# mLSTM cell and cosine-gated MLP on one core: the upper half of each w_in piece sent by GpSimd's queue

## The chip, the cores and the metric

One core of one Trainium2 chip runs the whole kernel in one launch. The metric is device time in microseconds. In the profile PE is TensorE, PEld its weight loads, DVE is VectorE, ACT is ScalarE, POOL is GpSimd and SP is SyncE, which here only issues DMAs; SPq and POOLq are the instruction queues of SP and GpSimd. L171 is line 171 of the kernel before; the change moves no line.

## The reference

Two blocks follow each other. The first is an mLSTM cell over 4 batches, 8 heads, 768 steps and a head size of 40:

```python
for t in range(S):
    m_new = np.maximum(f[t] + m, i[t])
    f_stab, i_stab = np.exp(f[t] + m - m_new), np.exp(i[t] - m_new)
    C = f_stab * C + i_stab * outer(v[t], k[t]);  n = f_stab * n + i_stab * k[t];  m = m_new
    y[t] = sigmoid(o[t]) * (C @ q[t]) / np.maximum(np.abs(n @ q[t]), 1.0)
```

The second takes the result as 3072 tokens of 320 features: `h = x @ w_in` (320 by 2048), `g = h * cos(h)`, `out = g @ w_out` (2048 by 320). The two weight matrices arrive as 64-bit floats, so the kernel loads each number as a pair of 32-bit words and makes a 32-bit float of it.

## The kernel before, in words

The sequence is cut into 6 chunks of 128 steps; with 4 batches that makes 24 cells, n = 4c + b for chunk c and batch b. A cell loads its q, k and v, forms scores (L481), weighs them with decay factors E (L404, L487), multiplies with values and state (L507 to L516), normalizes and turns the result (L525 to L536) into xT, the token features with features on partitions; the last 64 of the 320 features go into a second tile, xL, by two GpSimd DMAs for each cell of chunks 1 to 5 (L605). When a chunk of xT is whole, the MLP's first product, `Up(c, f2)`, runs for f2 = 0 to 7: four matmuls a half on xT with `w_in_sb` (L648) and one on xL with `w_in_l` (L642), into PSUM tiles pup; then the cosine gate on ACT and DVE (L656 to L668) and the second product (L680 in chunk 0, L758 later).

The order on every engine is written out by hand. `first_cells` sets up the gates and runs the cells of chunk 0; `both_parts(c, b)` then puts the MLP of chunk c beside the cells of chunk c + 1.

**How w_in comes in.** w_in is loaded in four pieces of 512 of its 2048 columns, by `weights_in(f)`, f = 0 to 3. A piece has two tiles of raw words. `bits` (partitions 0 to 127) takes 256 features, in four DMAs of 32 partitions, 256 KB each (L171). `low` takes the last 64 features, in four DMAs of 64 KB: two into partitions 0 to 63 and two into 64 to 127 (L176). All eight are issued by SP. Then `to_float32` converts: two ACT passes (L149, L151), three DVE passes (L155, L156, L162), one GpSimd pass that adds the two parts (L163), into `w_in_sb` (two slices of 512 columns) and `w_in_l`. w_out comes in eight pieces (L182) by the same conversion, as `w_out_sb`.

`weights_in(0)` stands in `first_cells` after the load of cell 3, `weights_in(1)` and `weights_in(2)` later in it, `weights_in(3)` in the first `both_parts`. A piece's instructions stand in the queue that issues them at that place, among that engine's other work. The tile `bits` has two buffers, shared with the decay factors of cell 3 (`E3`): piece 0 takes the second, piece 1 the first as soon as cell 3's value product (L497) has read E3, piece 2 the second again when piece 0 is converted, piece 3 the first. `low` shares two buffers with the first gates' tile in the same manner.

Other work on GpSimd that the steps below name: `kw`, the weighed keys (L409), needed by the state's increment on PE (L599); the triangular mask of E (L390), needed by the exponential on ACT (L400 or L404); `vr`, a copy of odd values (L415), and `qG`, the scaled queries (L463), both needed by the value product on PE (L510 to L516); the state's fade (L582); and the DMAs of the gates' tables to DRAM and back: `M_d` (L221, L247), `G_d` (L260), which SP reads again as E (L353) and G (L359).

SP's other loads are q and k (L326, L338), k and v for the state (L343), output gates o (L301, L308). A semaphore serves every eighth DMA of a kind of queue, so a DMA is issued when the eighth before it has landed; GpSimd's DMAs have eight such semaphores of their own.

Of the kernel before, what the change touches and what calls it, by code (L numbers as in the profile page):

```python
# [29 lines left out]
def kernel(  # L30
# [20 lines left out]
    nc = tc.nc  # L51
# [114 lines left out]
    w_in_last = moe_w_in.bitcast(I32).rearrange("(h d) (a e n) -> e a h d n", d=D, e=2, n=2 * 128)[:, :, :, 32:D]  # L166

    def weights_in(f):
        bits = pb.tile([128, NK, WP, 2], I32, name="bits", tag="bits")
        for a in range(HP):  # L170
            nc.sync.dma_start(out=bits[32 * a:32 * a + 32].rearrange("r i n two -> r i (n two)"),  # L171
                              in_=w_in_heads[a, 0:32, :, ts(f, 2 * WP)])
        low = p2.tile([128, 2 * 128, 2], I32, name="low", tag="S")
        for e in range(2):
            for a in range(2):
                nc.sync.dma_start(out=low[64 * e:64 * e + 64, ts(a, 128)].rearrange("r n two -> r (n two)"), in_=w_in_last[e, 2 * f + a])  # L176
        return [(w_in_sb[:, i, ts(f, WP)], bits[:, i]) for i in range(NK)] + [(w_in_l[:, ts(f, 2)].rearrange("p a n -> p (a n)"), low)]


# [652 lines left out]
    def first_cells():  # L832
# [29 lines left out]
        load_o(0, (2, 3))  # L862
        load(3)
        pieces.extend(weights_in(0))
        wall_in(1, 0, psum_o())
        wall_in(1, 1, psum_o())
# [55 lines left out]
        to_float32(pieces.pop(0))  # L922
        decay_exponents(B)
        pieces.extend(weights_in(1))
        outs.extend((p, weights_out(p)) for p in range(1, 3))
        seam_out(2)
# [15 lines left out]
        state(3)  # L942
        load_E(B + 2)
        ahead.append(weights_in(2))
        decay(B)
        sigmoid(1)
# [158 lines left out]
```

## Time and profile before

| | |
|---|---|
| median of 3 runs | 539.55 us (538.5 to 540.12) |
| the profiled execution: its time, its span | 540.26 us, 538.5 us |
| PE busy | 522.8 us (97%) |
| DVE busy | 419.5 us (78%) |
| ACT busy | 287.1 us (53%) |
| POOL busy | 247.8 us (46%) |
| hardware DMA queue (q1) | 96240 packets, 55.64 MB |
| software DMA queue (q0) | 1424 packets, 1.49 MB |

The time of the profiled execution is 1.8 us longer than its span, for what lies around it. The hardware queue is what SP issues (and one DMA of ACT), the software queue what GpSimd issues. Every part of w_in is loaded and converted in the first 119 us of the span; after that the change touches no instruction.

### The profile page before, as it was taken

To read this page: it belongs to the slowest core of one execution; us is meant where nothing else is said; L and a number is where in the kernel's file an instruction comes from. 1 tells how busy PE (TensorE), PEld (TensorE's weight loads), DVE (VectorE), ACT (ScalarE), POOL (GpSimd) and SP (SyncE) were. 2 spreads that over 40 slices of the span, in tenths; PEclk is the share of its full clock that TensorE was granted. 3 is DMA by queue.
4 is the path that set the end of the run, shared out by engine and by line. 5 is a ranking of instruction groups with operands and counts; after the bars stand their busy time and mean duration, and the time that the engine had idled before them with its cause. 6 is when DMAs were issued, how large, how long until landed. Compare 5 with 4: busy or idle time off the path is not lost.

```text
span 538.5 us, 10486 instructions
## 1 busy us (share of the span) xinstructions
PE 522.8 (97%) x3844; PEld 354.4 (66%) x3844; DVE 419.5 (78%) x907; ACT 287.1 (53%) x546; POOL 247.8 (46%) x409
## 2 busy tenths in 40 slices
PE   7999979999999999999999999999999999999996
PEld 4885536556666757767767767767657667576755
DVE  5565879897888988898878898878898879663636
ACT  2587949767566537827527826527836522222221
POOL 7435465465665865553553553553432433121211
PEclk9585989999999999999999999999999999999999
DMA  9999969799727539229249229159220000000001
GB/s 137 210 197 231 254 176 179 200 194 215 131 94 174 58 94 193 51 87 194 34 125 175 38 91 195 28 124 167 44 83 7 1 5 6 20 30 1 1 0 49
DMA packets 97762, 57.81 MB, mean 107 GB/s; under 512 B 62048, under 2 KB 89792, under 8 KB 97712
## 3 DMA queue, kind: packets, MB, share of 16 engines
q1 hardware_dynamic: 96240, 55.64, 50.4%
q0 software_dynamic: 1424, 1.49, 1.3%
q8 instruction: 30, 0.49, 0.4%
q14 instruction: 20, 0.16, 0.1%
q10 hardware_dynamic: 48, 0.02, 0.0%
HBM read 51.71 MB, written 4.11 MB: 104 GB/s over the span
## 4 chain that ended last, share of the span: by engine, by line
PE 76%; DMA 10%; DVE 8%; SPq 3%; POOL 2%; ACT 1%; issue 1%; DVEq 0%; POOLq 0%
PE pup L648 27%; PE acc L758 22%; PE pup L642 8%; PE po L680 5%; PE ps L481 3%; DMA bits<-in_moe_w_in_dram 3%; PE late L758 3%; PE vt L516 2%; PE vt L507 2%; DVE t L454 1%; DMA low<-in_moe_w_in_dram 1%; PE pu L599 1%; DMA G<-G_d 1%; DMA bits<-in_moe_w_out_dram 1%; DVE g L668 1%; DMA E<-M_d 1%
## 5 line engine op out<-in xcount | busy, mean ns | idle before, releaser
L648 PE MATMUL pup<-xT,w_in_sb 128*128 128x512 f32 x384 | 178.3, 607 | 4.0 <-POOL w_in_sb L163 2.9
L656 ACT ACTIVATE n<-pup 128x512 int32<-128x512 f32 x96 | 54.1, 595 | 201.7 <-PE pup L642 148.8
L648 PEld LDWEIGHTS pup<-xT,w_in_sb 128*128 128x128 f32 x384 | 70.7, 192 | 91.3 <-issue 84.4
L659 DVE SCALAR_TENSOR_TENSOR n<-pup,n 128x512 f32<-128x512 f32 x96 | 63.1, 687 | 79.6 <-ACT n L656 77.9
L722 POOL TENSOR_TENSOR D<-g 128x128 f32<-128x128 f32 x40 | 19.6, 490 | 138.0 <-DVE g L668 138.0
L664 ACT ACTIVATE n<-n 128x512 f32<-128x512 f32 x96 | 59.3, 630 | 16.0 <-DVE n L659 16.0
L668 DVE SCALAR_TENSOR_TENSOR g<-pup,n 128x512 f32<-128x512 f32 x96 | 62.0, 685 | 2.4 <-ACT n L664 1.7
L758 PE MATMUL acc<-w_out_sb,g 128*128 128x160 f32 x320 | 58.6, 304 | 0.0
L758 PE MATMUL acc<-T,g 128*128 128x160 f32 x320 | 58.0, 301 | 0.1
L642 PE MATMUL pup<-xL,w_in_l 64*128 64x512 f32 x192 | 55.7, 651 | 0.6 <-POOL w_in_l L163 0.6
L605 POOL DMA_DIRECT2D xL<-xT x40 | 22.4, 561 | 72.6 <-DVE xT L536 68.6
L758 PEld LDWEIGHTS acc<-w_out_sb,g 128*128 128x128 f32 x320 | 47.8, 190 | 5.6 <-issue 3.9
L758 PEld LDWEIGHTS acc<-T,g 128*128 128x128 f32 x320 | 48.1, 190 | 3.7 <-issue 3.0
L404 ACT ACTIVATE E<-E,tab 128x128 f32<-128x128 f32 x160 | 49.0, 389 | 0.3
L680 PE MATMUL po<-w_out_sb,g 128*128 128x320 f32 x128 | 36.2, 436 | 0.0
L481 PEld LDWEIGHTS ps<-t,t 40*128 40x128 f32 x384 | 26.4, 198 | 13.5 <-DVE t L454 7.2
L758 PE MATMUL acc<-T,S 128*128 128x160 f32 x160 | 35.0, 301 | 0.0
L680 PEld LDWEIGHTS po<-w_out_sb,g 128*128 128x128 f32 x128 | 24.0, 190 | 11.2 <-issue 1.9
L487 DVE TENSOR_TENSOR E<-ps,E 128x512 f32<-128x512 f32 x48 | 30.7, 681 | 0.5 <-PE ps L481 0.5
L642 PEld LDWEIGHTS pup<-xL,w_in_l 64*128 64x128 f32 x192 | 15.0, 187 | 24.5 <-issue 21.3
L481 PE MATMUL ps<-t,t 40*128 40x128 f32 x384 | 28.7, 289 | 1.1 <-DVE t L454 0.8
L758 PE MATMUL acc<-w_out_sb,S 128*128 128x160 f32 x160 | 28.8, 299 | 0.0
(177 smaller groups left out, 908.6 us busy)
## 6 DMA issues: line engine op xcount, KB each, us to landing
E<-M_d SPq DMA_DIRECT2D x22, 512.0 KB, 3.7
qr<-in_q_dram SPq DMA_DIRECT2D x36, 160.0 KB, 3.5
kr<-in_k_dram SPq DMA_DIRECT2D x36, 160.0 KB, 5.7
G<-G_d SPq DMA_DIRECT2D x20, 256.0 KB, 6.6
bits<-in_moe_w_out_dram SPq DMA_DIRECT2D x8, 640.0 KB, 6.8
bits<-in_moe_w_in_dram SPq DMA_DIRECT2D x16, 256.0 KB, 6.9
out_dram<-o_sb SPq DMA_DIRECT2D x24, 160.0 KB, 1.9
ks<-in_k_dram SPq DMA_DIRECT2D x10, 320.0 KB, 7.9
```

Source lines behind the costliest of these rows:

```text
L404: nc.scalar.activation(out=Es[n][:, h], in_=Es[n][:, h], func=AF.Exp, scale=-1.0, bias=tab[:, c, 0, g:g + 1])
L481: nc.tensor.matmul(ps[j][:, p], kT[r, p], qT[r, p], start=True, stop=True)
L487: nc.vector.tensor_tensor(out=w, in0=pss[n][j], in1=w, op=OP.mult)
L605: nc.gpsimd.dma_start(out=xL[c][64 * e:64 * e + 64, b], in_=ys[n][0:128:2])
L642: nc.tensor.matmul(pu, w_in_l[r, f2], xL[c][r].rearrange("p b t -> p (b t)"), start=ahead, stop=not ahead)
L648: nc.tensor.matmul(pu.rearrange("p (b t) -> p b t", b=B), w_in_sb[:, i, ts(2 * f2 + e, 128)], xT[c][:, i:NK * B:NK], start=(i == 0 and not ...
L656: nc.scalar.activation(out=self.n[e], in_=self.pu[e], func=AF.Copy, bias=0.25)
L659: nc.vector.scalar_tensor_tensor(out=self.n[e].bitcast(FP), in0=self.pu[e], scalar=0.25, in1=self.n[e], op0=OP.add, op1=OP.subtract)
L664: nc.scalar.activation(out=r, in_=r, func=AF.Sin, scale=TWO_PI_DOWN)
L668: nc.vector.scalar_tensor_tensor(out=g, in0=self.pu[e], scalar=TWO_PI, in1=self.n[e].bitcast(FP), op0=OP.mult, op1=OP.mult)
L680: nc.tensor.matmul(po[c][b], gs[c, f][:, ts(b, C)], w_out_sb[:, f], start=(f == 0), stop=(f == NF - 1))
L758: nc.tensor.matmul(a, lhs, rhs, start=start, stop=stop)
```

## The change

Of each piece, the `bits` DMAs with a = 2 and 3 (partitions 64 to 127) and the `low` DMAs with e = 1 (partitions 64 to 127) are issued by GpSimd instead of SP. Nothing else is edited. In the built program the order of PE, DVE and ACT stays as it was. SP has 16 DMAs less, GpSimd 16 more, four for each piece.

```diff
     def weights_in(f):
         bits = pb.tile([128, NK, WP, 2], I32, name="bits", tag="bits")
         for a in range(HP):
-            nc.sync.dma_start(out=bits[32 * a:32 * a + 32].rearrange("r i n two -> r i (n two)"),
+            (nc.sync, nc.gpsimd)[a // 2].dma_start(out=bits[32 * a:32 * a + 32].rearrange("r i n two -> r i (n two)"),
                               in_=w_in_heads[a, 0:32, :, ts(f, 2 * WP)])
         low = p2.tile([128, 2 * 128, 2], I32, name="low", tag="S")
         for e in range(2):
             for a in range(2):
-                nc.sync.dma_start(out=low[64 * e:64 * e + 64, ts(a, 128)].rearrange("r n two -> r (n two)"), in_=w_in_last[e, 2 * f + a])
+                (nc.sync, nc.gpsimd)[e].dma_start(out=low[64 * e:64 * e + 64, ts(a, 128)].rearrange("r n two -> r (n two)"), in_=w_in_last[e, 2 * f + a])
```

Where the four DMAs stand on GpSimd: piece 0's behind `kw` of cell 0 and ahead of the DMA of M_d (L247); piece 1's behind the mask of cell 4 (L390) and ahead of piece 0's second L163; piece 2's behind piece 0's third L163 and ahead of `kw`, `vr`, `qG` and the mask that follow; piece 3's behind the L163 of w_out's second piece and ahead of `qG`, `kw` and the mask.

## The prediction

> **What bounds the kernel now.** I read the page first: busy times and the chain that ended last.
>
> ```profile
> PE 522.8 (97%) x3844; PEld 354.4 (66%) x3844; DVE 419.5 (78%) x907; ACT 287.1 (53%) x546; POOL 247.8 (46%) x409
> PE 76%; DMA 10%; DVE 8%; SPq 3%; POOL 2%; ACT 1%; issue 1%; DVEq 0%; POOLq 0%
> ```
>
> PE is busy 97% of the span, so the change can at most act on 15.7 us of idle PE and on stretches at half clock. The waits of PE put its idle time almost wholly ahead of 75 us: 3.8 us before the first matmul, 2.9 us at 71.3 us (for L163 of w_in_sb), 0.9 us at 68.4 us. Later no gap is over 0.6 us. But DMA has 10% of the chain, so next the chain in order of time, in its first 75 us:
>
> ```profile
> 25.02 7.36 DMA low<-in_moe_w_in_dram
> 33.07 6.96 DMA G<-G_d
> 40.61 0.68 ACT w_in_sb L149
> ...
> 47.57 5.78 DMA bits<-in_moe_w_in_dram
> 53.36 6.79 DMA bits<-in_moe_w_out_dram
> 60.17 11.73 DMA bits<-in_moe_w_in_dram
> 71.93 0.70 DVE w_in_sb L162
> 72.77 1.33 POOL w_in_sb L163
> 74.14 2.56 PE pup L648 x4
> ```
>
> By this, w_in's transfers set the first PE gap. I don't take it on trust: does DVE stand still for a DMA at 71.9? Its timeline:
>
> ```profile
> 70.79 0.29 DVE L156 TENSOR_SCALAR w_in_l<-w_in_l 128x256 int32<-128x256 int32 x1
> 71.00 0.49 DVE L155 TENSOR_SCALAR w_out_sb<-w_out_sb 128x640 f32<-128x640 f32 x1
> 71.53 0.49 DVE L156 TENSOR_SCALAR w_out_sb<-w_out_sb 128x640 int32<-128x640 int32 x1
> 71.93 0.68 DVE L162 SCALAR_TENSOR_TENSOR w_in_sb<-bits,w_in_sb 128x512 int32<-128x512 int32 x1
> ```
>
> No idle time is noted: DVE runs instruction on instruction from 55.07, so L162 started when L156 let it. The words it reads (piece 1's) had been read by ACT's L149 from 68.23 on; the transfer at 60.17 is one of piece 2, which ACT reads first at 81.29. The DMA links are guesses of the chain. Behind DVE stands ACT, with no gap over 0.3 us from 46.30 to 71.5, and ACT began at 46.30 on PE's transposes, which waited for DVE's y and that for PE's L497 (39.73 to 43.37, at half clock). This is a chain of arithmetic.
>
> When do w_in's words come, against their first reader? Last `bits` issue plus the median time to landing of that piece's stretch: piece 0 23.7 + 7.3 = 31.0, ACT reads at 37.22; piece 1 48.9 + 5.8 = 54.7, read at 63.11; piece 2 60.2 + 13.1 = 73.3, read at 81.29; piece 3 78.8 + 6.4 = 85.2, read at 103.13. Each is 6 to 18 us early.
>
> **The change, part by part.** *SP loses 16 issues* (bits 0.43 us, low 0.60). SP is ahead of its readers, so sending w_in sooner gains nothing, nor do the loads behind it: ACT, DVE and PE show no wait for one of them. Value taken 0; bounds: a gain of the two PE gaps, 2.9 + 0.9 = 3.8 us, if the chain's DMA links are true after all, to no loss.
>
> *The engines that move the data* are busy 0.99 of 14 to 76 us (0.62 to 1.4 in the 10 us before). A second queue brings no bandwidth; it reorders. Piece 0's upper half, 2 x 256 + 2 x 64 = 640 KB, is now issued at 10.7 us instead of 23 to 27. At the 211 GB/s that 14 to 24 us shows, it pushes SP's loads there back by about 3 us until SP reaches its own, shorter, half. Nearest in need: q and k of cell 3, issued by 21.48, used on PE at 31.41; E of cell 2, issued at 13.12, used at 25.92. At the 5.6 us to landing that 12 to 15 us shows, they are there by 27.1 and 18.7: slack 4.3 and 7.2 us, so 0. M_d (L247, 16.04) now stands behind this half in GpSimd's queue; its reader E (L353) is issued at 31.85, and M_d landed in 5.7 us: 10 us of slack, so 0.
>
> *GpSimd gains 16 issues*, and this is where it could cost, because they stand in order among work that PE and ACT need. Price: a bits DMA from GpSimd is not in this trace. The nearest rows are xL's 40 issues (64 rows each, as bits has), M_d's (160 rows) and G_d's (80):
>
> ```profile
> L605 POOL DMA_DIRECT2D xL<-xT x40: 542/564/634, 64.8 to 453.7; - x40
> ```
>
> M_d took 0.65 us, G_d 0.55: hardly more for 160 rows than for 64. I take 0.58, 2.3 us a piece. Lower bound 0.31 (the least of SP's bits issues), upper bound 2.3, the longest SP was held by one such load (L326 at 19.17). Now what the 2.3 us displace:
>
> ```profile
> 9.65 1.05 POOL L409 TENSOR_TENSOR kw<-ks,tab 128x512 f32<-128x512 f32 x1
> 16.04 0.65 POOL L247 DMA_DIRECT2D M_d<-kr  x1 [5.33 <-DVE kr L245]
> ...
> 46.63 1.28 POOL L163 TENSOR_TENSOR w_in_sb<-w_in_sb,bits 128x512 int32<-128x512 int32 x1 [4.53 <-DVE w_in_sb L162]
> 48.99 0.73 POOL L163 TENSOR_TENSOR w_in_l<-w_in_l,low 128x256 int32<-128x256 int32 x1 [1.07 <-DVE w_in_l L162]
> 49.69 1.04 POOL L409 TENSOR_TENSOR kw<-ks,tab 128x512 f32<-128x512 f32 x1
> ...
> 76.85 1.27 POOL L463 TENSOR_TENSOR qG<-t,G 128x512 f32<-128x512 f32 x1
> ```
>
> - Piece 0: 10.7 to 13.0, inside the 5.33 us that POOL waits for DVE. Cost 0; at the upper bound 10.7 + 9.2 = 19.9, and M_d has slack.
> - Piece 1: the first issue waits for PE's last read of E3, L497's end at 43.37 (SP waited there too, which blocked SP alone). Behind it on POOL stands L163 of 46.63, idle until then for DVE. 43.4 + 2.3 = 45.7: cost 0, 0.9 us to spare there. PE needs that result only in the second half of its pup run, 46.83 + 6.02/2 = 49.8, so the issues may cost (49.84 - 1.28 - 43.4)/4 = 1.29 us each before PE feels it.
> - Piece 2: 49.7 to 52.0, and kw, vr, qG, the mask and two memsets move back by 2.3. qG ends at 54.5 instead of 52.2; PE takes it at 57.28 (L516). The mask ends at 55.5, ACT takes it at 60.76. kw is taken at 58.84. The memsets end at 57.8; L163 follows at 60.78. Cost 0; tips at (57.28 - 49.72 - 2.5)/4 = 1.26 us an issue.
> - Piece 3: 76.9 to 79.2. qG ends at 80.5, PE takes it at 84.57; the mask ends at 82.6, ACT takes it at 85.22; kw 81.5, taken at 85.89. Cost 0; tips at (85.22 - 76.9 - 3.4)/4 = 1.23.
>
> Later xL DMAs wait for semaphores that w_in's DMAs now hold, but by then these have long landed (piece 1's, issued at 43.4, before the xL of 64.84). Sum: 540.26 + 0 = 540.26 for the profiled execution, which lay 0.7 above the median of the runs shown; against that median the forecast is 539.6.
>
> Could DVE hold GpSimd's issues? In the trace the xL pair at 64.84 ran under DVE's L156 (64.91) and L162 and took 0.63 and 0.56 us, as the other pairs did. The only w_in issues under such DVE work are piece 1's (L155 and L156 from 44.88, L162 to 46.48). Held to the end of all three, they end at 46.48 + 2.3 = 48.8 and L163 at 50.1, 0.3 us after PE's 49.84. The Trainium skill, "SBUF — State Buffer", section on the two physically separate sides, warns of this: VectorE in a two-port mode locks GpSimd out of writing descriptors, and such a DMA of some 620 ns took some 3100. By that figure, an estimate, two held issues put PE 2.2 us late: 541.8.
>
> **The rivals.**
>
> *Dear issues (slower).* GpSimd makes the descriptors of a 256 KB load at more than xL's price. It decides from 1.23 to 1.29 us an issue on, at three places at once. At 2.0 us: piece 1 ends at 51.4, its two L163 at 53.4, piece 2 at 61.4, qG at 63.9 against 57.28: PE 6.6 us late; then piece 3's mask 88.3 against 85.22, 3.1 more. 540 + 9.7 = 549; at 1.6 us (qG 60.7, mask 86.7) 3.4 + 1.5, so 545. For it: no row has 4 KB rows on this queue. Against: 64 and 160 rows cost the same. Chance 0.22.
>
> *The chain is right (faster).* w_in's and w_out's transfers do set the 71 us gap; half a piece by a second queue comes earlier and the gaps at 68 and 71 close: 539.6 - 3.8 = 535.8, or 537.5 if half of it. For it: the chain's lines. Against: DVE's timeline, and engines at 0.99. Chance 0.14.
>
> *Held issues (the page's rule).* Piece 1's four issues wait for DVE's three passes as worked out above: 0.3 us, 539.9. For it: their place, from 43.4 on, beside L155. Against: the xL pair at 64.84. Chance 0.05.
>
> *The clock.* PE's granted clock was 0.50 in 14 to 24 us, and in 40 to 50; the stretches flip with how busy PE was shortly before. A small shift of any load could move one. L648 took 6.02 us for 8 matmuls at 46.83 and 3.65 later: 2.4 us of a flip, either sign. 537.2 or 542. Chance 0.06 faster, 0.10 slower.
>
> That the change doesn't do what it says is excluded by the built order: only SP's and GpSimd's differ.
>
> **How the numbers follow.** Forecast (nothing displaced) 0.43, held issues 0.05, which is also too little to measure, dear issues 0.22, chain right 0.14, clock 0.06 and 0.10: faster 0.20, same 0.48, slower 0.32. About 0.3% (1.6 us) is what a measurement can tell from no change. The forecast's own range is 538 to 541.2. For 8 in 10 it reaches down to 536.3, a little over the chain's full 535.8, and up to 546, which takes in dear issues to 1.6 us but not 2.0.
>
> **What would show it.** Right: L171 and L176 on POOL at 0.5 to 0.7 us each; the L163 at 46.6, PE's L507 near 57 and its pup near 74.1 as before; bytes of the software queue up by 2.6 MB; PE's gap of 2.9 us still there with DVE busy through it. Dear issues: L171 on POOL over 1.2 us and PE's L516 waiting for POOL qG. Chain right: pup starting before 72. Wrong in a way I have not priced: PE, DVE or ACT waiting for a DMA of SP in 14 to 40 us, which would mean that piece 0, sent early, displaced a load with less slack than I read.

## The result and the profile after

The change costs 9 to 10 us. In a first set of runs the changed kernel took 548.89 us (median of 4 runs, 541.84 to 550.94) beside 539.31 us for the kernel before on the same chip: ratio 1.0135, 95% interval 1.0091 to 1.0178. The ratio leaves out the run of 550.94, which counts as a slow one. The run of 541.84 makes the interval wide. A second set gave 549.51 us (548.48 to 550.46, 4 runs) beside 539.14 us, ratio 1.0196 (1.0175 to 1.0217). The profiled execution took 549.73 us with a span of 547.9 us, 9.4 us more than the 538.5 us before. The forecast was 539.6 us in a range of 536.3 to 546.0.

The page of the changed kernel, its busy times, its two large DMA queues and its chain by engine:

```profile
PE 518.8 (95%) x3844; PEld 350.7 (64%) x3844; DVE 419.9 (77%) x907; ACT 286.5 (52%) x546; POOL 257.5 (47%) x425
...
q1 hardware_dynamic: 95024, 53.02, 48.4%
q0 software_dynamic: 2448, 4.12, 3.8%
...
PE 72%; DVE 11%; ACT 6%; DMA 4%; SPq 2%; POOL 2%; issue 1%; DVEq 0%; ACTq 0%; POOLq 0%
```

The software queue is up by 2.6 MB, as it should be. PE is busy 4 us less and idle 13.4 us more (547.9 - 518.8 = 29.1 us against 15.7). Where the idle time lies, the waits of PE in the first 110 us say (engine, line, what it waited for: us in total, times, longest):

```profile
PE vt L507 <- issue: 14.4, 1, 14.4
...
PE pup L648 <- POOL w_in_sb L163: 2.2, 1, 2.2
```

It is one new wait of 14.4 us, before the value product of cell 4 (L507). The gap before pup that the chain of before had put down to w_in's transfers is still there, 2.2 us. For the new wait, ACT's timeline (start, duration, line, operation; in brackets the idle time before it):

```profile
43.88 0.75 ACT L623 COPY st<-pu 40x128 f32<-40x128 f32 x4
44.66 2.45 ACT L404 ACTIVATE E<-E,tab 128x128 f32<-128x128 f32 x8
60.83 1.28 ACT L317 ACT_TABLE_LOAD   x1 [13.73 <-DMA low<-in_moe_w_in_dram]
62.12 1.06 ACT L317 ACTIVATE og<-o 128x1024 f32<-128x1024 f32 x1
```

The table load (ACT_TABLE_LOAD) is the instruction that stands ahead of the sigmoid of L317. In the profile of before the same one began at 51.65 us, without idle time in front of it:

```profile
51.65 1.28 ACT L317 ACT_TABLE_LOAD   x1
```

Now ACT comes to it at 47.1 us, 4.5 us sooner, and stands 13.73 us. L317 is the sigmoid of the output gates; it reads o, not low. The name behind the arrow is a guess, taken from what ended last. In the trace the last of the eight o loads landed at 60.54 us, 0.29 us ahead of the table load; before it was 49.78. The chain in order of time names o:

```profile
41.10 0.65 PE px L592 x4
43.86 0.69 SPq L353
46.20 12.80 DMA o<-in_o_gate_dram
...
60.83 1.28 ACT L317
```

What stood in the way of o shows on GpSimd's timeline, where w_in's new issues are, each line two of them:

```profile
39.74 1.17 POOL L171 DMA_DIRECT2D bits<-in_moe_w_in_dram  x2
40.90 1.19 POOL L176 DMA_DIRECT2D low<-in_moe_w_in_dram  x2
...
45.18 1.12 POOL L171 DMA_DIRECT2D bits<-in_moe_w_in_dram  x2
46.30 1.18 POOL L176 DMA_DIRECT2D low<-in_moe_w_in_dram  x2
```

They cost 0.54 to 0.62 us each, as forecast. But piece 1's upper half is on its way from 39.74 us, piece 2's from 45.18, while SP was held in issuing E of cell 5 (L353) from 40.55 to 44.55 us and sent its o loads only from 44.60 on. Before, SP sent o ahead of piece 1 and both ahead of piece 2, because all stood in one queue. SP's timeline of the changed kernel, then of the kernel before:

```profile
40.55 4.00 SPq L353 DMA_DIRECT2D E<-M_d  x1
44.60 8.72 SPq L308 DMA_DIRECT2D o<-in_o_gate_dram  x8
```

```profile
42.90 3.93 SPq L308 DMA_DIRECT2D o<-in_o_gate_dram  x8
...
47.57 1.75 SPq L171 DMA_DIRECT2D bits<-in_moe_w_in_dram  x4
```

The DMA view of 42 to 47 us in the changed kernel (packets, MB, share of the 16 engines' time) shows the two queues at once:

```profile
DMA packets 2077, 0.76 MB, mean 153 GB/s; under 512 B 1965, under 2 KB 1965, under 8 KB 2077
q1 hardware_dynamic: 1915, 0.31, 62.2%
q0 software_dynamic: 162, 0.46, 60.0%
```

In these 5 us each queue takes about as much of the engines' time as the other, and SP's loads, nearly all in packets under 512 bytes, move only 0.31 MB in it. In 42 to 50 us the changed kernel moved 168 GB/s and the kernel before 240, all of it from SP's queue. The second queue is not the only thing that lowers such a rate: the run before_o_early below, where SP's queue is the only one at work in 42 to 47 us, moved 159 GB/s there, with 4068 of its 4258 packets under 512 bytes.

### The profile page after: what moved, and what is told of

Its sections match the earlier page's. It is cut to its first block, busy times and chain, and to the rows that moved or that the text cites. A ratio compares the mean times of both kernels' runs of the same rounds, so it can differ in the third digit from the quotient of the medians.

```text
span 547.9 us, 10493 instructions
## 1 busy us (share of the span) xinstructions
PE 518.8 (95%) x3844; PEld 350.7 (64%) x3844; DVE 419.9 (77%) x907; ACT 286.5 (52%) x546; POOL 257.5 (47%) x425
## 4 chain that ended last, share of the span: by engine, by line
PE 72%; DVE 11%; ACT 6%; DMA 4%; SPq 2%; POOL 2%; issue 1%; DVEq 0%; ACTq 0%; POOLq 0%
PE pup L648 25%; PE acc L758 22%; PE pup L642 8%; PE po L680 3%; PE ps L481 3%; PE late L758 3%; DMA o<-in_o_gate_dram 2%; PE vt L516 2%; PE vt L507 2%; DVE g L668 2%; DVE n L659 2%; DVE t L454 1%; PE pu L599 1%; PE ph L497 1%; SPq L301 1%
## 5 line engine op out<-in xcount | busy, mean ns | idle before, releaser
L656 ACT ACTIVATE n<-pup 128x512 int32<-128x512 f32 x96 | 54.1, 595 | 201.7 <-PE pup L642 148.9
L481 PEld LDWEIGHTS ps<-t,t 40*128 40x128 f32 x384 | 24.9, 188 | 13.1 <-DVE t L454 7.3
L507 PE MATMUL vt<-E,vs 128*32 128x128 f32 x320 | 17.1, 286 | 14.4 <-issue 14.4
```

What stands on the lines that cost most here:

```text
L481: nc.tensor.matmul(ps[j][:, p], kT[r, p], qT[r, p], start=True, stop=True)
L507: nc.tensor.matmul(vt[32 * a:32 * a + 32, i], vs(n)[:, h, 0:32], E[:, h], start=True, stop=False)
L656: nc.scalar.activation(out=self.n[e], in_=self.pu[e], func=AF.Copy, bias=0.25)
```

## The experiments

The theories to tell apart are these. A: w_in's halves, sent by a queue that is not held, get ahead of the loads that SP still has to send, and ACT's L317 waits for o. A has two versions: the order alone does it (A1), or the second queue also lowers the rate (A2). Q: a second, software queue costs by itself, whenever it is used. Beside them, C: the semaphores of every eighth DMA hold the last o loads back; D: chance of PE's clock.

The column that matters in each is the start of the table load ahead of L317 on ACT, and the idle time in front of it.

**One piece at a time.** In the first, piece 2 is sent by SP alone, so that piece 1 is the dose; in the second the other way round; in the third only pieces 0 and 3 use GpSimd's queue.

```diff
-            (nc.sync, nc.gpsimd)[a // 2].dma_start(...)
+            (nc.sync, nc.gpsimd)[a // 2 if f in (0, 1, 3) else 0].dma_start(...)   # p2_on_sp
+            (nc.sync, nc.gpsimd)[a // 2 if f in (0, 2, 3) else 0].dma_start(...)   # p1_on_sp
+            (nc.sync, nc.gpsimd)[a // 2 if f in (0, 3) else 0].dma_start(...)      # p03_on_gps
```

(and `low` likewise). Expected of p2_on_sp:

> Pieces 0, 1 and 3 as in the change, piece 2 wholly by SP. Theory A (the upper halves of pieces 1 and 2, 640 KB each on GpSimd's queue, move ahead of and between the gate loads o, so ACT's sigmoid L317 waits; here half of that is gone): o lands at 54 to 57 us instead of 60.5, ACT's wait ahead of L317 falls from 13.7 to 7 to 10 us, time 542 to 546. Theory C (the last two o loads are issued late, at 51 and 53 us, because SP must wait for the eighth DMA before, vs and E, which piece 1's half has delayed; piece 2 hardly matters): time stays 547 to 549. Theory D (chance of PE's clock): 548 or 540, without relation to o.

Expected of p1_on_sp:

> Pieces 0, 2 and 3 as in the change, piece 1 wholly by SP. Theory A: piece 2's half alone still goes ahead of o: o lands at 53 to 56 us, time 541 to 545. Theory C: vs and E land as before, SP issues all eight o by 46.5 us, time 539 to 541. Theory D: no relation.

Expected of p03_on_gps:

> Only pieces 0 and 3 as in the change, pieces 1 and 2 by SP. Theories A and C both: o lands near 50 us, no wait of ACT ahead of L317, 538 to 541. If GpSimd's issues as such cost time (the dear issues of the prediction), half of the loss stays: 543 to 546.

Measured beside 539.07 us: p2_on_sp 544.37 (ratio 1.0101, 1.0072 to 1.0131), p1_on_sp 542.06 (1.0039, 1.0013 to 1.0065), p03_on_gps 539.33 (1.001, 0.9988 to 1.0031). ACT's timeline of p2_on_sp, then of p1_on_sp:

```profile
56.39 1.28 ACT L317 ACT_TABLE_LOAD   x1 [9.25 <-DMA o<-in_o_gate_dram]
```

```profile
54.06 1.28 ACT L317 ACT_TABLE_LOAD   x1 [6.66 <-DMA o<-in_o_gate_dram]
```

Pieces 0 and 3 cost nothing, so what the prediction worked out for them held. Piece 1 alone costs 5.3 us, piece 2 alone 3.0 (its 10 runs lie between 537.99 and 543.91), both together 9 to 10, somewhat over the sum of 8.3. In p2_on_sp the last o load was issued at 54.12 us, right behind E of cell 5 landing at 54.10: theory C is true as a part of A, since E was late for the same reason. That piece 2 hardly matters was wrong.

**The o loads out of the way.** The whole change, with the eight o loads moved on SP ahead of k, v and E:

```diff
+        load_o(1)
         load_two(B, "Kv")
         load_E(B + 1)
-        load_o(1)
```

> The whole change, and SP's eight o loads moved ahead of the loads of k and v for cell 4 (L343), which wait for PE. Theories A and C: o is issued by 37 us and lands by 46, ACT's L317 follows L404 at once; the loss shrinks to what comes late next (w_out's first piece, which landed at 64.6 us in the changed kernel, and E of cell 5): 539 to 544. If something else than o holds ACT at 47 to 60.8 us: 547 to 549.

541.63 us (539.56 to 543.25, 10 runs), ratio 1.0045 (1.0023 to 1.0068): most of the loss is gone, not all. The runs fall in two groups, 539.6 (four) and 541.5 to 543.3 (six). The profiled one, 539.63, is of the first: o landed at 44.1, the table load began at 51.55 without a wait. Expected of another run, for a profile of the second group:

> The changed kernel with the o loads early, once more, for a profile of its other group of runs (539.6 and 541.5 to 543.3). If it falls in the second group: ACT or PE waits 2 to 4 us for E of cell 5, w_out's first piece or k and v, which then stand behind GpSimd's halves; if it falls in the first group: as before, no wait at L317.

It took 542.25 us. Its table load begins at 47.30 us, 4.2 us earlier, without a wait; then come these, on ACT's and on PE's timeline:

```profile
59.68 0.80 ACT L149 ACTIVATE w_out_sb<-bits 128x640 f32<-128x640 f32 x1 [6.05 <-DMA bits<-in_moe_w_out_dram]
```

```profile
55.65 0.66 PE L507 MATMUL vt<-E,vs 128*32 128x128 f32 x8 [5.72 <-DMA vs<-in_v_dram]
```

Whatever stands behind the halves in SP's queue is late: o in the changed kernel; v (landed 55.5) and w_out's first piece (59.66) once o is out of the way.

**Later on the same queue.** The whole change, but GpSimd's issues of piece 1 stand ahead of two memsets (53 us) and those of piece 2 behind w_out's first L163 (62 us). The main lines of the edit, shortened; `half` issues one half of a piece on the queue that it is given:

```diff
+        half(0, nc.sync)
+        upper.update({f: half}) if f in (1, 2) else half(1, nc.gpsimd)
...
+                        upper.pop(1)(1, nc.gpsimd); clear_low()
...
+                    next_out(...); b == 0 and upper.pop(2)(1, nc.gpsimd)
```

> The whole change, but GpSimd issues its halves of pieces 1 and 2 later: piece 1's at about 53 us (ahead of two memsets), piece 2's at about 62 us (behind w_out's first L163). The queue, the bytes and the number of issues are the changed kernel's; only the moment differs. Theory A (sent while SP is held, the halves go ahead of and between the o loads): o lands near 50 as before, the table load ahead of L317 stands near 51.6 with no wait, time 538.5 to 541; w_in's words are still there before ACT reads them at 63 and 81. Theory Q (a second, software queue on the same engines costs by itself, whenever it is used): about what the changed kernel loses, 547 or more. A third outcome, 541 to 545 with a new wait for piece 1's or w_out's words at 58 to 66 us, would say that the halves find no free place at all.

541.46 us (538.39 to 541.89, 10 runs) beside 539.49, ratio 1.0033 (1.0012 to 1.0054). Q falls: the same queue with the same bytes loses 2 us instead of 9 to 10. The time is a little above what theory A gave, and the third outcome, late words of w_in, is there in part. o landed at 50.62 and L317 does not wait; instead, on ACT's timeline (here L317 is L318):

```profile
51.52 1.28 ACT L318 ACT_TABLE_LOAD   x1
...
63.97 0.68 ACT L149 ACTIVATE w_in_sb<-bits 128x512 f32<-128x512 f32 x1 [0.94 <-issue]
```

Piece 1's upper words, issued at 53.05, landed at 61.79 and 63.90, just ahead of that L149: now they are late, by 0.94 us, half of the 2 us. The other half stays unexplained.

**A smaller dose.** GpSimd issues only `bits` with a = 3 of each piece:

```diff
-            (nc.sync, nc.gpsimd)[a // 2].dma_start(...)
+            (nc.sync, nc.gpsimd)[a // 3].dma_start(...)
```

> A smaller dose: GpSimd issues one DMA of each piece's eight (bits with a = 3, 256 KB), SP the other seven. Theory A: 512 KB of pieces 1 and 2 instead of 1280 KB ahead of o; at 180 to 200 KB/us that is 2.6 to 2.8 us for o, against the 3.2 us between o's landing and its reader in the kernel before: 539 to 542, and L317's wait under 3 us. Theory Q (any use of a second queue here): 545 or more. If bytes count in proportion, 9.6 x 0.4 = 3.8: 543.

539.81 us (538.2 to 542.36, 10 runs), ratio 1.0017 (0.9998 to 1.0037): too little to tell from no change, and less than in proportion. In its profile o landed at 50.95 us, with the table load at 51.59; that is an execution in which ACT comes late (granted clock 0.51 in 14 to 28 us), so it does not show whether ACT would wait for o in an early one. The same holds for the profile of p03_on_gps.

**No second queue at all.** The kernel before, all of w_in by SP, with the o loads behind w_out's first piece and piece 1 instead of ahead of them; and the kernel before with SP itself sending the upper half of piece 1 ahead of E and o, ahead of the same loads that the half of p2_on_sp overtook (the other pieces' upper halves also go first there, directly followed by their lower halves):

```diff
-        load_o(1)
...
         pieces.extend(weights_in(1))
+        load_o(1)                       # before_o_late
```

```diff
         load_two(B, "Kv")
+        piece1 = weights_in(1)          # sp_half_first: only its upper half is issued here
         load_E(B + 1)
         load_o(1)
...
-        pieces.extend(weights_in(1))
+        pieces.extend(piece1); lower.pop()(0)
```

Expected of before_o_late:

> No second queue: the kernel before, with the eight o loads moved on SP behind the eight loads of piece 1 (and w_out's first). Order alone then puts 1.28 MB of w_in and 0.64 MB of w_out ahead of o, more bytes than the changed kernel puts ahead of it (2 x 640 KB). Theory A1 (order alone is the loss): o lands near 57 to 61 and the time is 545 to 550. Theory A2 (the second queue also lowers the rate at which o's 640-byte rows move): at the 250 KB/us that the kernel before shows there, 1.9 MB are through in about 7.7 us behind 47, so o lands near 55 to 57, and ACT loses 3 to 5 us: 542 to 545.

Expected of sp_half_first:

> One queue, the order of two: SP itself issues the upper half of piece 1 (640 KB) ahead of E of cell 5 and the o loads; the lower half and all else stay where they are in the kernel before. p2_on_sp sent the same 640 KB at the same place by GpSimd's queue: E of cell 5 landed at 54.1 us, o at 56.1, 544.4 us. If order alone is what costs (theory A1), E and o land as late as there, near 54 and 56, and the time is 543.5 to 545. If the second queue costs beyond the order (theory A2), 640 KB at the 240 KB/us of the kernel before push E and o back by 2.7 us and the issues by 2.2: E lands near 49 to 51, o near 52 to 54, time 540 to 543.

before_o_late: 546.72 us beside 539.49, ratio 1.0162 (1.0128 to 1.0196). sp_half_first: 543.94 (543.27 to 544.16) beside 539.14, ratio 1.0088 (1.0073 to 1.0104). ACT's timeline of the first, then of the second (there L317 is L318):

```profile
59.08 1.28 ACT L317 ACT_TABLE_LOAD   x1 [11.87 <-DMA o<-in_o_gate_dram]
```

```profile
55.75 1.28 ACT L318 ACT_TABLE_LOAD   x1 [4.21 <-DMA o<-in_o_gate_dram]
```

So one queue makes such a loss too, with no second queue in play: 640 KB ahead of E and o cost 4.8 us by SP and 5.3 by GpSimd, and the intervals overlap. Both times lie where A1 put them. The landings of sp_half_first lie between the two versions: E at 51.8 and o at 55.5, against 54.1 and 56.1. Its loss is not bytes alone, though. SP waited for L497, sent the half from 43.36 us and its first o load at 46.32, 3.4 us later than the 42.90 of the kernel before; in p2_on_sp GpSimd sent the half from 40.00 us and SP its first o load at 42.44. The rates may speak for something of A2: in 40 to 56 us p2_on_sp moved 150 GB/s and sp_half_first 191. What part of the loss the order has and what part the rate is not settled.

**Was o on the edge before?** Two runs of the kernel before: once more as it is, and with the o loads early (the edit of o_early, without the change).

> The kernel before again, for a profile in which the half clock falls elsewhere. Where the arithmetic is 4.5 us earlier than in the first profile (table load ahead of L317 near 47.1 instead of 51.65), theory A says that ACT waits for o here too, until about 49 to 50: 2 to 3 us of idle time at L317 that the first profile does not show. Time 536 to 540.

> The kernel before with the eight o loads moved on SP ahead of the k, v and E loads of cell 4; all of w_in by SP. In the kernel before nothing waits for o, so theory A says no change: 538.2 to 540.2, o landed near 44. If the rest of 2.5 us that the same move left in the changed kernel (541.6 against 539.1) comes from k, v and E standing behind o, it shows here too: 541 to 542. If it comes from the halves that GpSimd sends, it doesn't.

before_again took 539.27 us. On its ACT timeline:

```profile
45.00 2.45 ACT L404 ACTIVATE E<-E,tab 128x128 f32<-128x128 f32 x8
52.30 1.28 ACT L317 ACT_TABLE_LOAD   x1 [4.85 <-DMA o<-in_o_gate_dram]
```

So ACT waits for o in the kernel before as well, 4.85 us, in an execution whose arithmetic is 4.2 us earlier. PE's granted clock was 0.51 in 14 to 28 us of the first profile and 1.00 in this one (1.00 in the changed kernel's too); in the first profile ACT came later than o, behind matmuls at half clock, so no wait showed. before_o_early: 538.75 us (536.88 to 541.16, 12 runs) beside 539.49, ratio 0.9996 (0.9976 to 1.0017). The profiled run, of 536.88, has the early arithmetic and the table load at 47.17 without a wait, but over all runs the gain is too small to tell from none; no version here beats the kernel before.

**The changed kernel again:**

> The changed kernel again, for its spread (541.8 to 549.7 so far): theory A says that the loss depends on when GpSimd's issues of piece 1 get past L497, at 39.7 us where the clock put the arithmetic early or at 43.4 where it did not. Expected: most runs 547 to 551, some at 541 to 543; median 547 to 550, ratio 1.012 to 1.018.

Its times stand with the result. Its profile is like the first: table load at 60.37 us behind 13.35 us of idle time, o landed at 60.08. No run near 541.8 came, and the one of the first set has no profile: why it was some 7 us shorter stays open.

**One row for all.** The time of a profiled run less the start of its table load ahead of L317 is 488.6 in the first profile of before, 487.0 in before_again, 488.9 and 488.1 in the changed kernel, 488.2 in p2_on_sp, 488.4 in p1_on_sp and sp_half_first, 487.1 in before_o_late, 488.1 in o_early, 488.0 in p03_on_gps, 489.7 in before_o_early; the ends are 486.6 (one_of_eight) and 490.3 (late_place). Only o_early_again, with its later waits, lies outside (495.0). The start of that one instruction moved from 47.2 to 60.8 us, and the time with it.

## Why the prediction was wrong

*The step that failed is the term of the engines that move the data.* It said that a second queue brings no bandwidth but reorders, which the runs bear out, and then priced only piece 0, whose half goes out at 10.7 us. For pieces 1 and 2 it asked when w_in's own words are read (there they have 6 us and more) and when GpSimd's and PE's work behind the issues is due, but not what SP still had to send behind those bytes. The sum needed the term: 640 KB of piece 1 and 640 KB of piece 2 ahead of o. At the 240 GB/s of 42 to 50 us that is 2.7 us each; from before_again's 52.2 us of landing, piece 1 pushed o to 56.1 (3.9 us) and piece 2 on to 60.5 (4.4 us). At 2.7 us each the term alone, less the 1.9 us that o came ahead of ACT in the first profile, would have given 543, still inside the range. The rest is that the pushes were larger, 8.3 us for 5.4, and that in the changed kernel ACT came at 47.1 us, so that nothing covered them. The pushes fit the lower rate (168 GB/s in 42 to 50 us) and E's late landing, which held the last o load; how much each of the two has no run tells.

*"SP loses 16 issues": the value of sending sooner was right, its argument was not.* "ACT, DVE and PE show no wait for one of them" was read in one execution. There o landed at 49.78 us and ACT came at 51.65, 1.9 us later; in before_again, where the clock was 1.00 in 14 to 28 us, ACT comes at 47.4, and o is 4.8 us late. I weighed the clock as a gain or loss of 2.4 us, not as something that uncovers a wait.

*"It waits for PE's last read of E3, L497's end at 43.37 (SP waited there too, which blocked SP alone)."* I took the place of these issues as a cost to GpSimd alone. It is what reorders: in the changed kernel L497 ended at 38.85 us and GpSimd sent piece 1 at 39.74, directly behind the mask (L390), while SP was held in the issue of E until 44.55. Nor did SP wait there for L497 in the kernel before: its issue of E lasted until 42.85, the eight o loads stood next, and it came to piece 1 at 47.57, 4.2 us after L497's end. Those o loads are what piece 1 was behind and now is not.

*GpSimd's issues.* 0.58 us was right (0.54 to 0.62), 2.3 us a piece too, so the rival of dear issues falls by its own sign: L171 stays far under 1.2 us. What stood behind the issues on GpSimd was hardly late for them: L163 of `w_in_sb` ran from 42.11 us, 0.15 behind the end of DVE's L162. Piece 2's issues ended at 47.5, and `vr` (L415) waited then 2.57 us for v, a load. So the tipping points never came into play.

*The chain is right.* The gap before pup is still 2.2 us (2.9 before), with half of each piece sent by another queue, and no run here is clearly faster. It falls. *Held issues:* DVE's three passes (L155, L156, L162) ran from 40.35 to 41.96 us beside the issues of piece 1, and none of these took over 0.62 us; it falls. The lock that the Trainium skill's "SBUF — State Buffer", section "SBUF: two separate sides", tells of does not show in the duration of an issue here. *The clock* fell differently in these executions, as the prediction held possible, but it is not the loss: p2_on_sp, with 0.76 in 14 to 28 us, and sp_half_first, with 0.51, took about the same time.

*The range.* It ended at 546.0 because dear issues at 1.6 us gave 545. The cause that the runs show had no case; the sentence on what would make the forecast wrong named the kind (an engine that waits for a DMA of SP, displaced), but put it at 14 to 40 us and at piece 0.

## What to carry to other kernels

Moving DMAs to a second queue changes their place in the order, even if the program's order on each engine is untouched: what the old queue held back behind a wait now goes at once, and its bytes lie ahead of every load that the old queue still has to send. For each moved transfer, list the loads that it was behind and now is not, take bytes over the measured rate, and set that against each load's own slack. Read the slack in more than one execution; where the granted clock shifts, a load that seems early may be covered by slow matmuls.

## What the hardware showed

- A queue of small rows keeps a share of the engines' time beside one of large rows, but moves little in it: in 42 to 47 us of the changed kernel SP's queue had 62.2% and moved 0.31 MB, GpSimd's 60.0% and 0.46 MB. The shares are not fixed: 55.1% and 62.2% in the second profile of the changed kernel, 45.0% and 72.6% in p2_on_sp. The Trainium skill, "DMA: Bandwidth & Descriptors", section "Queues, rings and completion order", says that each engine goes round between the queues packet by packet, a packet being several descriptors; the first shares, with 1915 packets of the profile for SP and 162 for GpSimd, would fit turns of some 12 small rows against one large, but the turns themselves no trace here shows. For SP's loads 0.31 MB in 5 us is 62 GB/s; alone, with larger rows among them, they had 240 in 42 to 50 us of the kernel before, and alone with small rows 159 in 42 to 47 us of before_o_early.
- A late load holds others back: E of cell 5 was issued from 40.55 us and landed at 52.99 in the changed kernel, 12.4 us later, and since a DMA waits for the one eight before it, the last o load went out at 53.01, 5.8 us behind the sixth.
- In executions of the same kernel the full and half clock fell differently: 0.51 or 1.00 in 14 to 28 us. ACT's arrival at L317 moved with it by 4.2 us (51.65 or 47.4), yet the time of the kernel before by only 1.0 us (540.26 and 539.27), as the wait for o took most of it. The stretch at half clock can lie later, too: late_place has 0.96 in 14 to 28 us, 0.50 in 42 to 50, and ACT comes at 51.5. What decides where the half clock falls these runs do not show.
